# Reading four accumulators at once at the end of a block, in a kernel of a causal convolution and a two-layer squared-ReLU network on one core

## The chip, the core and the metric

One Trainium2 chip, one of its cores. The metric is the device time of one execution in microseconds (us). TensorE (PE) multiplies matrices and writes into PSUM, VectorE (DVE) and ScalarE (ACT) do elementwise work and alone of the engines used here read PSUM, GpSimd (POOL) does a few additions and maxima over partitions, SyncE (SP) and ACT start transfers. Each engine runs its own instructions in their written order and waits for others by semaphores.

## The reference

```python
def _attn_ref(x, weight):             # x (8, 4096, 192), weight (8, 7)
    w = exp(weight - max(weight)); w = w / (sum(w) + 1e-09)
    x_pad = zeros of 6 tokens in front of each sequence, then x
    out[b, s, h, g] = sum over k of w[h, k] * x_pad[b, s + k, h, g]
def _moe_ref(x, w_in, w_out, s, b):   # x (32768, 192), w_in (192, 2048), w_out (2048, 192)
    h = x @ w_in
    r = maximum(h, 0)
    return (s * (r * r) + b) @ w_out
```

A causal convolution of seven taps over the tokens (one set of taps for each of 8 groups of 24 features), and behind it a network with 2048 hidden features whose activation is a scaled square of the ReLU plus an offset.

## The kernel before, in words

Features lie on partitions, tokens along the free dimension. 192 features are 128 ("A") and 64 ("B"). The 32768 tokens are 32 superblocks `n` of 1024 tokens, each two blocks `j` of 512. A block has eight steps `p`, one for each pair of 128 hidden features. All products need nearly full float32 precision, so each operand is split into a high part that TensorE takes exactly and a low rest.

A step has a first layer (`firsts`, L595: 18 matmuls on half of the rows each, two at a time, into the PSUM tile `h`, of which there are two), ACT's ReLU (L627) and square (L634), DVE's cast to the high part `qh` (L643) and DVE's rest (L647 in superblocks 0 and 1; from superblock 2 on, the constant `OLD`, L659, kept in float16). Steps are put into a queue, and the second layer of a step (`second`: L813 in superblock 1, L864 from superblock 2 on) is issued `LAG` = 2 steps behind its first layer. From superblock 2 on the second layer takes only the high parts of the activations; their float16 rests are multiplied once for a block, when its eight steps are through: `rest_B` (L879, 32 matmuls) and `rest_A` (L891, 64 matmuls). These sum into the same four PSUM accumulators of a block, `accs[0]` and `accs[2]` for the A outputs, `accs[1]` and `accs[3]` for the B outputs, and the next block's second layer uses the same four banks: it can't start before they are read.

They are read in `end_of_block`: for B, an ACT instruction (L910) and three DVE instructions (L914), for A one of ACT (L919) and one of DVE (L920). The A tokens of the next block, meanwhile, come from the convolution: DVE multiplies and adds seven taps (L185, L187), ACT copies the high part (L221), DVE subtracts it (L214) and SP swaps the halves of the result with two transfers (L197, L198) into `wA` or `wB`. This work is a generator, cut into pieces, and `convolve(k)` issues the next k of them: `pace` says how many in each step, and `end_of_block` issues three between `rest_B` and the reading of B, and two between `rest_A` and the reading of A. A piece for a tile that is still being read is held back by a gate. If tokens aren't ready when their block begins, `need` issues what is missing on the spot. Each superblock also needs the largest absolute token (L676, then POOL's L673) for its scale, and five small DVE instructions (`unit_of_tokens`).

Superblock 2 is special: before its second layer can run, the second weights `W` are scaled in place (`scale_pair`, L707) and rounded to float16 (`halve_pair`, L712, L713), and its scale needs the column sums and the largest weights that are found in superblock 1 (`column_sums`, `largest_in`, `largest_out`, L557, L676). The outputs of superblocks 0 and the first block of superblock 1 get their bias later (`add_bias`, L583).

Of the kernel before, what the change touches and what calls it, by code (L numbers as in the profile page):

```python
# [15 lines left out]
ALU = mybir.AluOpType  # L16
# [37 lines left out]

RING = 12

WINDOW = 5

GAP = 160

# [15 lines left out]
def conv_attention_then_squared_relu_mlp(  # L76
# [729 lines left out]
    def second_split(n, j, p, qh, ql):  # L806
        accs = accumulators(n, j, p)


        def both(to, w, f, q, start=False, stop=False, cols=P):  # L810
            for i in range(2):
                r = slice(i * HB, (i + 1) * HB)
                nc.tensor.matmul(  # L813
                    accs[to + 2 * i][0:cols], w(f, r), q[r, f % 2, :],
                    start=start and f == 0, stop=stop and f == NF - 1,
                )

        both(1, w_outB, 2 * p, qh, start=True)
        both(1, hiB, 2 * p, ql, cols=HIS)
        both(1, hiB, 2 * p + 1, ql, cols=HIS)  # L820
        both(1, w_outB, 2 * p + 1, qh, stop=True)
        for f in (2 * p, 2 * p + 1):
            both(0, loA, f, qh, start=True)
            both(0, hiA, f, qh)
            both(0, hiA, f, ql, stop=True)
        if p == NPAIR - 1:
            t0 = n * SUP + j * BLK
            early = (n, j) == (1, 0)

            o = {k: hold(n, j, k) for k in range(2)}  # L830
            for k, name in ((1, "oB"), (0, "oA")):
                o[k + 2] = out_tile(name + "2")
                nc.scalar.activation(
                    o[k], accs[k], AF.Identity, scale=sb, bias=0.0 if early else bias[:, k : k + 1]
                )
                nc.scalar.activation(o[k + 2], accs[k + 2], AF.Identity, scale=sb)
            nc.gpsimd.tensor_tensor(o[1], o[1], o[3], op=ALU.add)

            oC = out_tile("oC")[0:DB]
            nc.sync.dma_start(oC, o[1][DB:P])  # L840
            nc.gpsimd.tensor_tensor(o[0], o[0], o[2], op=ALU.add)
            toA, toB = outT[0:P, t0 : t0 + BLK], outT[P:D, t0 : t0 + BLK]
            oB = o[1][0:DB] if early else oC
            if not early:
                nc.sync.dma_start(toA, o[0])
            nc.gpsimd.tensor_tensor(oB, oC, o[1][0:DB], op=ALU.add)
            if early:
                unbiased.extend(((o[0], toA, 0), (oB, toB, 2)))
            else:
                nc.sync.dma_start(toB, oB)  # L850
            del acc[n, j]
# [46 lines left out]
    def next_out():  # L898
        turn[0] += 1
        return out_tile(room[turn[0] % 6])  # L900

    def end_of_block(n, j):

        t0 = n * SUP + j * BLK
        scale = units(n)[1]
        accs = acc[n, j]
        rest_B(n, j)
        convolve(WINDOW - 2)
        oB = next_out()[0:DB]
        nc.scalar.activation(  # L910
            oB, accs[1][DB:P], AF.Identity, scale=scale[DB:P], bias=bias[DB:P, 1:2]
        )
        for a in (accs[1][0:DB], accs[3][0:DB], accs[3][DB:P]):
            nc.vector.scalar_tensor_tensor(oB, a, scale[0:DB], oB, op0=ALU.mult, op1=ALU.add)  # L914
        nc.sync.dma_start(outT[P:D, t0 : t0 + BLK], oB)
        rest_A(n, j)
        convolve(2)
        oA = next_out()
        nc.scalar.activation(oA, accs[0], AF.Identity, scale=scale, bias=bias[:, 0:1])  # L919
        nc.vector.scalar_tensor_tensor(oA, accs[2], scale, oA, op0=ALU.mult, op1=ALU.add)  # L920
        nc.sync.dma_start(outT[0:P, t0 : t0 + BLK], oA)
        del acc[n, j]

    def end_of_last():
# [107 lines left out]
            if next(stream) == "gated":  # L1032
                raise ValueError(what)

    def pace(j, p):
        return 2 if p in (2, 3 + 2 * j) else 1

    steps = [(n, j, p) for n in range(NSUP) for j in range(2) for p in range(NPAIR)]

    def step(n, j, p):  # L1040
        now[0] = 16 * n + 8 * j + p
# [5 lines left out]
            else:  # L1047
                need(n, "A", 1)
        h = first(n, j, p)
        put(n, j, p, squares(h, nc.vector.tensor_copy, *(units(n)[:1] if n >= OLD else ())))  # L1050
        if (n, j) == (1, 1):
            if p < NPAIR - 1:
                column_sums(p + 1)
            largest_out(p)
            convolve(1)
        elif n == 1:
            largest_in(p)
            convolve(2 + p % 2)
        else:
            convolve(pace(j, p))  # L1060
        if (j, p) == (1, NPAIR - 2) and OLD <= n + 1 < NSUP:
            if n + 1 > OLD:
                unit_of_tokens(n + 1)
        if (n, j) == (OLD, 0):
            scale_pair(p)
        if n == OLD and 0 < 8 * j + p <= NPAIR:
            halve_pair(8 * j + p - 1)
        if (n, j, p) == (1, 1, NPAIR - 1):
            unit_of_weights()
            unit_of_tokens(OLD)  # L1070
        if (n, j, p) == (2, 0, 0):
            biases()
        elif n == 2 and p % 2 == 0 and unbiased:
            add_bias()
        if (n, j, p) == steps[-1]:
            return end_of_last()
        while queue and len(queue) > LAG + (
            queue[0][2] == 0 and queue[0][0] <= OLD and queue[0][:2] not in ((1, 0), (OLD, 1))
        ):
            item = queue.pop(0)  # L1080
            second(*item)
# [59 lines left out]
```

## Time and profile before

| | |
|---|---|
| median of 3 runs | 2367.63 us (2366.81 to 2372.58) |
| the profiled execution | 2368.6 us, its span 2366.8 us |
| mean granted TensorE clock | 0.968 of full speed |
| TensorE busy | 2234.1 us, 94% of the span |
| VectorE busy | 1775.0 us, 75% |
| ScalarE busy | 1302.0 us, 55% |
| GpSimd busy | 29.0 us, 1% |

Busy time is the time in which an engine has an instruction in work, summed over the span. A busy TensorE isn't one at its peak: with its clock at one half it is busy for twice as long. Times in the rows further down are counted from the start of the span.

### The profile page before, as it was taken

The numbers are of one execution on the slowest core, as the hardware profiler recorded it, in microseconds if no ns is written. First come the engines' busy times: TensorE is split into PE (matmuls) and PEld (weight loads), VectorE is DVE, ScalarE is ACT, GpSimd is POOL, SyncE is SP. The second block draws the span as 40 slices with busy tenths as digits, with TensorE's granted clock in tenths as the row PEclk, the third lists the DMA queues.
The fourth block names the chain that finished last, engine by engine and source line by source line (L and its number), as shares of the span: only waits on it lengthen the run. The fifth ranks groups of instructions, "written<-read, shape, count | busy, mean of one in ns | idle before, by whom it ended". The sixth has DMA issues, their size and how long they took to land.

```text
span 2366.8 us, 48136 instructions
## 1 busy us (share of the span) xinstructions
PE 2234.1 (94%) x21392; PEld 1766.4 (75%) x21392; DVE 1775.0 (75%) x2391; ACT 1302.0 (55%) x1322; POOL 29.0 (1%) x53
## 2 busy tenths in 40 slices
PE   8999899999999999999999999999999999999999
PEld 6777677777777777767778787786777877777776
DVE  7888678877777677777777777777777677777765
ACT  6747455555555555555455555555555555555554
POOL 0010000000000000000000000000000000000000
PEclk9999999999999999999999999999999999999999
DMA  4112111112112011120111211112112111121110
GB/s 157 32 30 68 42 51 50 48 37 55 39 55 55 19 53 48 46 55 26 46 48 45 55 30 41 51 42 55 32 39 55 39 55 41 30 55 39 50 33 15
DMA packets 41457, 110.00 MB, mean 46 GB/s; under 512 B 6816, under 2 KB 7072, under 8 KB 41248
## 3 DMA queue, kind: packets, MB, share of 16 engines
q1 hardware_dynamic: 32464, 83.03, 13.1%
q10 hardware_dynamic: 8784, 23.89, 3.5%
q8 instruction: 167, 2.74, 0.5%
q14 instruction: 42, 0.34, 0.0%
HBM read 31.66 MB, written 25.17 MB: 24 GB/s over the span
## 4 chain that ended last, share of the span: by engine, by line
PE 75%; DVE 15%; ACT 6%; issue 4%; DMA 1%; DVEq 0%; SPq 0%; POOL 0%; ACTq 0%; POOLq 0%
PE h L595 41%; PE acc L864 26%; PE acc L891 4%; DVE outs L914 3%; ACT q L627 3%; ACT q L634 3%; DVE acc L187 2%; PE acc L879 2%; DVE outs L920 2%; DVE few L676 2%; DVE ql L643 1%; DVE sA L214 1%; DVE sB L214 1%; DMA wA<-sA 1%; DVE acc L185 1%
## 5 line engine op out<-in xcount | busy, mean ns | idle before, releaser
L627 ACT ACTIVATE q<-h,few 128x1024 f32<-128x1024 f32 x480 | 536.5, 1118 | 776.8 <-PE h L595 773.2
L634 ACT ACTIVATE q<-q 128x1024 f32<-128x1024 f32 x512 | 542.9, 1060 | 16.1
L595 PE MATMUL h<-sA,W 64*128 64x512 f32 x3024 | 544.3, 406 | 5.2 <-DVE sA L214 3.8
L595 PE MATMUL h<-wA,W 64*128 64x512 f32 x3024 | 527.4, 395 | 4.0 <-DMA wA<-sA 3.8
L595 PE MATMUL h<-wB,W 64*128 64x512 f32 x1536 | 451.8, 402 | 0.0
L595 PE MATMUL h<-sB,W 64*128 64x512 f32 x1536 | 451.4, 402 | 0.0
L643 DVE CAST ql<-q 128x1024 fp32r<-128x1024 f32 x238 | 165.2, 694 | 364.1 <-ACT q L634 364.1
L595 PEld LDWEIGHTS h<-sA,W 64*128 64x128 f32 x3024 | 377.3, 191 | 73.6 <-issue 24.6
L595 PEld LDWEIGHTS h<-wA,W 64*128 64x128 f32 x3024 | 382.3, 191 | 52.4 <-DMA wA<-sA 7.5
L864 PE MATMUL acc<-qh,W 64*128 64x512 f32 x1920 | 335.4, 406 | 86.6 <-DVE outs L920 86.6
L864 PEld LDWEIGHTS acc<-qh,W 64*128 64x128 f32 x1920 | 231.2, 189 | 135.3 <-DVE outs L920 111.3
L595 PEld LDWEIGHTS h<-wB,W 64*128 64x128 f32 x1536 | 297.2, 194 | 26.1
L595 PEld LDWEIGHTS h<-sB,W 64*128 64x128 f32 x1536 | 298.3, 194 | 23.5 <-issue 0.4
L864 PE MATMUL acc<-ql,W 64*128 64x512 f32 x1900 | 303.4, 386 | 0.0
L659 DVE TENSOR_TENSOR q<-q,qh 128x1024 f16<-128x1024 f32 x240 | 294.1, 1225 | 8.2
L659 DVE TENSOR_TENSOR q<-q,ql 128x1024 f16<-128x1024 f32 x238 | 291.7, 1226 | 8.1
L643 DVE CAST qh<-q 128x1024 fp32r<-128x1024 f32 x251 | 174.6, 696 | 155.7 <-ACT q L634 151.8
L187 DVE SCALAR_TENSOR_TENSOR acc<-xA,share,acc 128x512 f32<-128x512 f32 x372 | 279.0, 750 | 5.4
L864 PEld LDWEIGHTS acc<-ql,W 64*128 64x128 f32 x1900 | 230.2, 184 | 25.0
L864 PE MATMUL acc<-qh,q 64*128 64x512 f32 x960 | 210.5, 398 | 21.5 <-DVE outs L914 21.3
L891 PE MATMUL acc<-q 64*64 64x512 f16 x3840 | 217.4, 376 | 0.0
L864 PE MATMUL acc<-ql,q 64*128 64x512 f32 x950 | 197.3, 389 | 0.0
(161 smaller groups left out, 1692.3 us busy)
## 6 DMA issues: line engine op xcount, KB each, us to landing
wA<-sA SPq DMA_DIRECT2D x124, 256.0 KB, 3.7
wB<-sB SPq DMA_DIRECT2D x62, 256.0 KB, 3.7
outT<-outs SPq DMA_DIRECT2D x59, 256.0 KB, 2.0
xA<-in_xA ACTq DMA_DIRECT2D x23, 515.0 KB, 3.5
outT<-outs SPq DMA_DIRECT2D x62, 128.0 KB, 2.3
xB<-in_xB ACTq DMA_DIRECT2D x30, 259.0 KB, 2.7
q<-in_w SPq DMA_DIRECT2D x7, 768.0 KB, 6.3
xA<-in_xA ACTq DMA_DIRECT2D x7, 512.0 KB, 3.6
```

What stands on the lines that cost most here:

```text
L187: nc.vector.scalar_tensor_tensor(acc, src, w[:, k : k + 1], acc, op0=ALU.mult, op1=ALU.add)
L214: nc.vector.tensor_tensor(s[:, 1, cols], acc, s[:, 0, cols].bitcast(F32), op=ALU.subtract)
L595: nc.tensor.matmul(h[:, i, :], w_in(w, p, chunk[0], rows), chunk[part], start=start, stop=stop)
L627: nc.scalar.activation(q, h, AF.Relu, scale=unit)
L634: nc.scalar.activation(at[0], at[0], AF.Square)
L643: cast(qh, q)
L659: nc.vector.tensor_tensor(ql, q, qh.bitcast(F32), op=ALU.subtract)
L676: nc.vector.tensor_reduce(to, of, axis=axis, op=ALU.max, apply_absolute_value=True)
L864: nc.tensor.matmul(accs[to + 2 * i], w(f, r), qh[r, f % 2, :], start=f == 0 and w is not hiA, stop=whole and f == NF - 1 and w is not loA, ...
L879: nc.tensor.matmul(accs[1 + 2 * k][c], half_B(2 * p + i)[r], ql[r, i, :], start=False, stop=p == NPAIR - 1, skip_group_check=True,)
L891: nc.tensor.matmul(accs[2 * k][c], half_A(f)[r, c], ql[r, f % 2, :], start=False, stop=f == NF - 1, skip_group_check=True,)
L914: nc.vector.scalar_tensor_tensor(oB, a, scale[0:DB], oB, op0=ALU.mult, op1=ALU.add)
```

## The change

At the end of a block `rest_A` follows `rest_B` without anything between, the output instructions come behind both, and one piece of the convolution stands ahead of the last of them, three after it. The other pieces go into the steps, by the table `PACE`. The queue holds the first step of each block for a step longer than before (all blocks but the first of superblock 1; before, that held only in the early superblocks). In superblocks 1 and 2, ACT makes the casts of odd steps. The second block of superblock 1 is read by ACT and DVE, no longer by ACT and POOL. The maxima of the weights, the float16 weights and the late biases move to other steps.

```diff
-WINDOW = 5
+HALVE = {2: (0,), 3: (1,), 4: (2, 3), 5: (4,), 6: (5,), 7: (6,), 8: (7,)}
+
+PACE = (1, 0, 0, 3, 1, 2, 1, 2)
...
-                nc.scalar.activation(o[k + 2], accs[k + 2], AF.Identity, scale=sb)
-            nc.gpsimd.tensor_tensor(o[1], o[1], o[3], op=ALU.add)
+                if early:
+                    nc.scalar.activation(o[k + 2], accs[k + 2], AF.Identity, scale=sb)
+                    nc.gpsimd.tensor_tensor(o[k], o[k], o[k + 2], op=ALU.add)
+                else:
+                    nc.vector.scalar_tensor_tensor(
+                        o[k], accs[k + 2], sb, o[k], op0=ALU.mult, op1=ALU.add
+                    )
...
-            nc.gpsimd.tensor_tensor(o[0], o[0], o[2], op=ALU.add)
...
         rest_B(n, j)
-        convolve(WINDOW - 2)
-        oB = next_out()[0:DB]
+        rest_A(n, j)
+        oB, oA = next_out()[0:DB], next_out()
         nc.scalar.activation(
             oB, accs[1][DB:P], AF.Identity, scale=scale[DB:P], bias=bias[DB:P, 1:2]
         )
         for a in (accs[1][0:DB], accs[3][0:DB], accs[3][DB:P]):
             nc.vector.scalar_tensor_tensor(oB, a, scale[0:DB], oB, op0=ALU.mult, op1=ALU.add)
         nc.sync.dma_start(outT[P:D, t0 : t0 + BLK], oB)
-        rest_A(n, j)
-        convolve(2)
-        oA = next_out()
         nc.scalar.activation(oA, accs[0], AF.Identity, scale=scale, bias=bias[:, 0:1])
+        convolve(1)
         nc.vector.scalar_tensor_tensor(oA, accs[2], scale, oA, op0=ALU.mult, op1=ALU.add)
         nc.sync.dma_start(outT[0:P, t0 : t0 + BLK], oA)
+        convolve(3)
...
-    def pace(j, p):
-        return 2 if p in (2, 3 + 2 * j) else 1
+    def pace(n, p):
+        return PACE[p] + (n == OLD and p in (0, 5))
...
+    def caster(n, p):
+        return nc.scalar.copy if n <= OLD and p % 2 else nc.vector.tensor_copy
...
         if (n, j) == (1, 1):
+            convolve(1)
             if p < NPAIR - 1:
                 column_sums(p + 1)
-            largest_out(p)
-            convolve(1)
+            if p < 4:
+                largest_in(p + 4)
+                largest_out(p)
+            elif p < 6:
+                largest_out(2 * p - 4)
+                largest_out(2 * p - 3)
         elif n == 1:
-            largest_in(p)
-            convolve(2 + p % 2)
+            convolve(3)
+            if p < 4:
+                largest_in(p)
         else:
-            convolve(pace(j, p))
+            convolve(pace(n, p))
...
-        if n == OLD and 0 < 8 * j + p <= NPAIR:
-            halve_pair(8 * j + p - 1)
-        if (n, j, p) == (1, 1, NPAIR - 1):
+        for k in HALVE.get(now[0] - 16 * OLD, ()):
+            halve_pair(k)
+        if (n, j, p) == (1, 1, NPAIR - 2):
             unit_of_weights()
             unit_of_tokens(OLD)
...
-        elif n == 2 and p % 2 == 0 and unbiased:
+        elif n == OLD + 1 and p % 2 == 0 and unbiased:
             add_bias()
...
         while queue and len(queue) > LAG + (
-            queue[0][2] == 0 and queue[0][0] <= OLD and queue[0][:2] not in ((1, 0), (OLD, 1))
+            queue[0][2] == 0 and queue[0][:2] != (1, 0)
         ):
```

What this does to the order, at three places. First TensorE behind the float16 run of a block in the middle of the program (the end of the second block of superblock 16; L891 and L897 are the last matmul of `rest_A`). Before:

```order
L891 MATMUL acc_14018<-q 64x512
L595 MATMUL h<-sA,W 128x512 x6
L595 MATMUL h<-wB,W 128x512
L595 MATMUL h<-sB,W 128x512
...
L595 MATMUL h<-wA,W 128x512 x6
L864 MATMUL acc_14441<-qh,q 128x512
L864 MATMUL acc_14443<-qh,q 128x512
```

and in the changed kernel, where L597 is the first layer and L870 the second:

```order
L897 MATMUL acc_14040<-q 64x512
L597 MATMUL h<-sA,W 128x512 x6
...
L597 MATMUL h<-wA,W 128x512 x6
L597 MATMUL h<-sA,W 128x512 x6
...
L597 MATMUL h<-wA,W 128x512 x6
L870 MATMUL acc_14462<-qh,q 128x512
L870 MATMUL acc_14464<-qh,q 128x512
```

The next block's second layer now begins after two groups of the first layer instead of one; the second layers of its first two steps then follow each other.

Second, VectorE at the same place. Before:

```order
L643 CAST ql<-q 128x1024
L659 TENSOR_TENSOR q<-q,ql 128x1024
L214 TENSOR_TENSOR sA<-acc,sA 128x512
L676 TENSOR_REDUCE few<-xA 128x1
L676 TENSOR_REDUCE few<-few 128x1
L185 TENSOR_SCALAR acc<-xA,share 128x512
L214 TENSOR_TENSOR sB<-acc,sB 128x512
L914 SCALAR_TENSOR_TENSOR outs<-acc_14441,few,outs 64x512
L914 SCALAR_TENSOR_TENSOR outs<-acc_14443,few,outs 64x512 x2
L187 SCALAR_TENSOR_TENSOR acc<-xA,share,acc 128x512 x2
L920 SCALAR_TENSOR_TENSOR outs<-acc_14442,few,outs 128x512
L643 CAST qh<-q 128x1024
```

and in the changed kernel (L920 and L924 read the accumulators, L216 is the low part, L678 the maximum, L187 the first tap):

```order
L645 CAST ql<-q 128x1024
L661 TENSOR_TENSOR q<-q,ql 128x1024
L920 SCALAR_TENSOR_TENSOR outs<-acc_14462,few,outs 64x512
L920 SCALAR_TENSOR_TENSOR outs<-acc_14464,few,outs 64x512 x2
L216 TENSOR_TENSOR sA<-acc,sA 128x512
L924 SCALAR_TENSOR_TENSOR outs<-acc_14463,few,outs 128x512
L678 TENSOR_REDUCE few<-xA 128x1
L678 TENSOR_REDUCE few<-few 128x1
L187 TENSOR_SCALAR acc<-xA,share 128x512
L216 TENSOR_TENSOR sB<-acc,sB 128x512
L645 CAST qh<-q 128x1024
L661 TENSOR_TENSOR q<-q,qh 128x1024
```

The three B readings come first, one low part stands ahead of the A reading, and the rest of the convolution's pieces follow it.

Third, VectorE ahead of superblock 2, whose first tokens are `sA`. Before, their low part stands behind the last column sums of superblock 1:

```order
L557 TENSOR_TENSOR sumA<-sumA,W 128x512
L557 TENSOR_TENSOR sumB<-sumB,WB 128x128
L560 TENSOR_TENSOR sumA<-sumA 128x256
L561 TENSOR_TENSOR sumA<-sumA 128x128
L562 TENSOR_TENSOR sumB<-sumB 128x64
L676 TENSOR_REDUCE few<-W 128x1
L676 TENSOR_REDUCE few<-q 128x1
L214 TENSOR_TENSOR sA<-acc,sA 128x512
```

In the changed kernel it stands ahead of the third of seven column sums (L559 is a column sum, L649 the rest of a step):

```order
L645 CAST qh<-q 128x1024
L649 TENSOR_TENSOR ql<-q,qh 128x1024
L216 TENSOR_TENSOR sA<-acc,sA 128x512
L559 TENSOR_TENSOR sumA<-sumA,W 128x512
L559 TENSOR_TENSOR sumB<-sumB,WB 128x128
L678 TENSOR_REDUCE few<-W 128x1 x2
L678 TENSOR_REDUCE few<-q 128x1
```

The low part moved up by four steps of superblock 1.

## Rows read from the trace of the kernel before

**Rows 1.** Who waited for whom, TensorE alone: total us, times, longest us.

```profile
PE acc L864 <- DVE outs L920: 86.6, 56, 2.1
PE acc L864 <- DVE outs L914: 21.3, 52, 0.7
```

**Rows 2.** Timeline at the end of a block: start, duration (us), engine, line [idle before].

```profile
1199.60 1.23 DVE L659 TENSOR_TENSOR q<-q,ql 128x1024 f16<-128x1024 f32 x1
1199.64 3.62 PE L891 MATMUL acc<-q 64*64 64x512 f16 x64
...
1200.75 0.68 DVE L214 TENSOR_TENSOR sA<-acc,sA 128x512 fp32r<-128x512 f32 x1
1201.35 1.22 DVE L676 TENSOR_REDUCE few<-xA 128x1 f32<-128x1030 f32 x1
...
1203.19 0.96 PE L595 MATMUL h<-sA,W 64*128 64x512 f32 x6
1203.30 0.78 ACT L919 ACTIVATE outs<-acc,bias,few 128x512 f32<-128x512 f32 x1 [2.68 <-PE acc L891]
1203.67 2.37 DVE L914 SCALAR_TENSOR_TENSOR outs<-acc,few,outs 64x512 f32<-64x512 f32 x3
...
1205.57 1.11 ACT L627 ACTIVATE q<-h,few 128x1024 f32<-128x1024 f32 x1 [1.49 <-PE h L595]
1205.96 1.52 DVE L187 SCALAR_TENSOR_TENSOR acc<-xA,share,acc 128x512 f32<-128x512 f32 x2
...
1206.18 0.70 PE L864 MATMUL acc<-qh,q 64*128 64x512 f32 x3 [0.43 <-DVE outs L914]
...
1206.71 1.06 ACT L634 ACTIVATE q<-q 128x1024 f32<-128x1024 f32 x1
1207.52 0.75 DVE L920 SCALAR_TENSOR_TENSOR outs<-acc,few,outs 128x512 f32<-128x512 f32 x1
1208.18 0.68 DVE L643 CAST qh<-q 128x1024 fp32r<-128x1024 f32 x1
...
1208.32 1.19 PE L864 MATMUL acc<-qh,W 64*128 64x512 f32 x7 [1.40 <-DVE outs L920]
```

**Rows 3.** Timeline of TensorE, one step in the last superblock.

```profile
2303.32 0.84 PE L595 MATMUL h<-sA,W 64*128 64x512 f32 x6
...
2305.36 0.62 PE L864 MATMUL acc<-ql,q 64*128 64x512 f32 x4
...
2306.72 0.84 PE L595 MATMUL h<-sA,W 64*128 64x512 f32 x6
```

**Rows 4.** Busy time of the engines in stretches of the span; PEclk is the granted clock.

```profile
core 0: us, PE busy (x) PEld busy (x) DVE busy (x) ACT busy (x) POOL busy (x), PEclk, DMA share, GB/s
123.50:160.20 36.70, 35.16 (x308) 27.71 (x306) 36.04 (x59) 19.87 (x22) 6.48 (x5) 1.00 0.10 26
95.55:210.76 115.21, 107.91 (x894) 85.06 (x894) 100.54 (x162) 68.71 (x87) 11.63 (x9) 0.96 0.17 45
210.76:2354.49 2143.73, 2031.09 (x19777) 1613.70 (x19776) 1591.90 (x2102) 1162.44 (x1148) 16.41 (x36) 0.97 0.16 44
2294.48:2327.21 32.73, 32.73 (x338) 25.12 (x338) 18.87 (x21) 18.98 (x19) 0.00 (x0) 1.00 0.11 29
1281.90:1285.30 3.40, 3.40 (x18) 2.71 (x16) 2.20 (x3) 0.00 (x0) 0.00 (x0) 0.50 0.14 54
162.27:170.23 7.96, 3.99 (x21) 2.04 (x19) 6.68 (x23) 0.06 (x1) 0.50 (x1) 0.72 0.26 66
```

**Rows 5.** Timeline of TensorE where superblock 2 begins.

```profile
164.83 0.73 PE L595 MATMUL h<-sA,W 64*128 64x512 f32 x4 [2.17 <-DVE sA L214]
```

**Rows 6.** Timeline of POOL and VectorE where superblock 1's last outputs are added.

```profile
183.46 1.73 POOL L841 TENSOR_TENSOR q<-q,outs 128x512 f32<-128x512 f32 x1
```

```profile
183.96 1.51 DVE L707 TENSOR_SCALAR W<-W,few 128x512 fp32r<-128x512 f32 x1
...
189.94 0.48 DVE L707 TENSOR_SCALAR W<-W,few 128x512 fp32r<-128x512 f32 x1
```

More of the change, by code (lines that the diff above doesn't have):

```diff
@@ L1049, in step @@
         h = first(n, j, p)
-        put(n, j, p, squares(h, nc.vector.tensor_copy, *(units(n)[:1] if n >= OLD else ())))
+        put(n, j, p, squares(h, caster(n, p), *(units(n)[:1] if n >= OLD else ())))
         if (n, j) == (1, 1):
+            convolve(1)
             if p < NPAIR - 1:
                 column_sums(p + 1)
-            largest_out(p)
-            convolve(1)
+            if p < 4:
[4 more added lines that the diff above has]
+                largest_out(2 * p - 3)
         elif n == 1:
-            largest_in(p)
-            convolve(2 + p % 2)
+            convolve(3)
+            if p < 4:
+                largest_in(p)
         else:
-            convolve(pace(j, p))
+            convolve(pace(n, p))
         if (j, p) == (1, NPAIR - 2) and OLD <= n + 1 < NSUP:
```

## The prediction, made before the changed kernel ran

> **What bounds the kernel now.** I read the waits first. TensorE's longest waits by far are for the two places that read the accumulators, 86.6 us for the A reading and 21.3 us for the B reading, in nearly every one of the 60 blocks of superblocks 2 to 31 [rows 1]. The timeline of one block end shows why [rows 2]. The float16 run of B ends at 1199.64, that of A at about 1203.19. VectorE is free for the B reading at 1200.83 (1199.60 + 1.23), but has pieces of the convolution to do first and begins it at 1203.67. For A, ScalarE's half is done at 1204.08, yet VectorE begins its half at 1207.52: the B readings (2.37) and two taps (1.52) stand ahead of it. TensorE gets on with the B half of the second layer at 1206.18 and with the A half at 1208.32.
>
> What a block costs without such a wait is seen at the end, where no tokens are left to convolve: from the first float16 matmul of block 30/1 to that of block 31/0 TensorE is busy for all of 32.73 us, at a granted clock of 1.00 [rows 4]. Over the 59 intervals between the first and the last such point the time is 2143.73 us, 36.33 for a block, and the granted clock 0.97 [rows 4]. So 59 x (36.33 - 32.73) = 212.7 us lie in waits and what they cause: 107.9 us are waits proper [rows 1]; the clock's missing 3% of 2143.73 us are some 64 us; the other 41 us are TensorE starting again after each pause, and a late start of superblock 3. The clock falls right behind a pause: 1281.90 to 1285.30 runs at 0.50, which is 1.2 GHz, after a block end, and the unbroken stretch at 2.4 GHz [rows 4]. I count the clock's loss as part of the pauses' price.
>
> VectorE is busy for 1591.90 us of those 2143.73 us, 26.98 for a block [rows 4]; in 32.73 us that would be 82%. ScalarE, 1162.44 us, would reach 60%. So TensorE should bound the middle of the program, if the other two come in time.
>
> Ahead of it the picture differs. Between 95.55 and 210.76 TensorE has 894 matmuls; at 2.04 us for 18 [rows 3], 0.113 each, that is 101.3 us of 115.21, so 13.9 us are lost here. But VectorE is busy for 100.54 us of it, and in 123.50 to 160.20 for 36.04 of 36.70 us [rows 4]: there VectorE is the bound.
>
> **The change: end of a block.** The order listing puts the three B readings directly behind the rest. With the durations of rows 2, counted on the same block: B is read from 1200.83 to 1203.20, still inside `rest_A`; the low part follows to 1203.88; ScalarE's A half runs from 1203.30 to 1204.08 as before, and VectorE's A half from there to 1204.85. TensorE has two groups of the first layer to do first, 2 x 2.04 us [rows 3], and comes to the second layer at 1203.19 + 4.08 = 1207.27. Spare: 2.4 us. The wait is gone, not shortened.
>
> What is late next? VectorE's casts. Behind the A reading stand the maximum (1.22), a small one, a first tap and a second low part (together under 2 us, by the 0.68 us of a low part, the longest of the three), so VectorE is free at about 1207.5; in the other variant of the order one more tap (0.75) makes that 1208.2. The ReLU of step 2 runs from 1205.57 to 1206.68, its square to 1207.77 [rows 2], so the cast ends at 1208.9 at worst, and TensorE wants it after two second layers (1.36 each, [rows 3]) and another first layer, at 1207.27 + 2.72 + 2.04 = 1212.0. Spare: 3 us. In step 3 the table puts three taps (2.3 us) behind a cast and a rest (1.9 us); that is 4.2 us in a step of 3.40 us, so the next cast slips by under a microsecond, and the steps behind it carry one or two taps. The queue one step longer costs no transfer and no instruction: it needs `qh` for three waiting steps, and there are six buffers.
>
> Fourteen pieces a block are now issued where fifteen were, and 13.5 are needed (27 for a superblock). By the listing the tokens for a block are ready six or seven steps ahead of it, so `need` has nothing left to do. The transfers on SP keep their order relative to VectorE's work, and each is wanted steps later.
>
> Sum for the 59 intervals: -212.7 us. Bounds: 0 if TensorE waits as long elsewhere, and 212.7 if it never waits.
>
> **The change: superblocks 1 and 2.** Superblock 2 began late because its tokens' low part stood behind all column sums: TensorE waited 2.17 us for it [rows 5] and then for the swap, and a group that takes 2.04 us lasted 7.96 us at a clock of 0.72 [rows 4]. The low part now stands four steps earlier. That stall of 5.9 us and the slow matmuls behind it go, with the cover of four steps of 4.3 us (38 matmuls each) for the swap.
>
> Against that, VectorE is full here. It loses 12 casts of odd steps in this stretch, 12 x 0.68 = 8.2 us [rows 2], and ScalarE, busy for 68.71 of 115.21 us [rows 4], has room for them (at the square's 1.06 us, 12.7 us). It gains two readings of accumulators, 1.5 us at the A reading's 0.75. POOL's three additions for superblock 1's last block go; while one of them ran, a scaling took 1.51 us where another took 0.48 [rows 6], so three such collisions give back about 3.1 us. VectorE's 100.54 us become some 90.7 us, in 101.3 us if TensorE never waited. That fits only if spread evenly, and the listing doesn't: until the scale of superblock 2 is known, nearly all of it stands in eight steps that were already full, and only four of the odd casts are in them. I take VectorE to reach superblock 2 about 3 us late, and the new readings of superblock 1's accumulators, behind a scaling and a rest, to hold TensorE for about 3 us more. Of 13.9 us I book 7.8, with 0 and 13.9 as bounds.
>
> The Trainium skill (SBUF — State Buffer, section "SBUF: two separate sides") says that VectorE and GpSimd share a pair of ports that one of them holds for a whole instruction while the other is blocked. By it each of the three additions would block for up to the 1.73 us of rows 6, some 5.2 us in all, and the sum would be 2 us lower. The row shows 1.03 us, which I use.
>
> The spread of `halve_pair` and the late biases move ScalarE work of the same length into steps where ScalarE is at most 60% busy; booked at nothing, and if that cover were gone, a bias instruction is under the 0.78 us of the A reading [rows 2], six times.
>
> **Sum.** The profiled execution took 2368.6 us, 1.8 us more than its span, and 1 us more than the median of the three runs, 2367.63. 2368.6 - 212.7 - 7.8 = 2148.1. I predict 2148 us, 9.3% less. Its own range is 2138 to 2165: lower if the early part loses nothing, higher if a block keeps 0.2 to 0.3 us.
>
> **Rivals.**
> *A part of the wait stays.* VectorE runs in order at 82%, and one late instruction delays a cast or a reading; the spare of 2.4 us is from one block. For it: VectorE's full stretch above. Against it: the listing repeats the same two orders. If half of what a block loses stayed, 2148 + 106 = 2254 us; at a quarter, 2201.
> *The clock stays.* If the pauses aren't what lowers it, 64 us remain: 2212 us. Against it, the last blocks run at 1.00 without pauses [rows 4]. The Trainium skill (TensorE: Matmul & The Clock Gate, "Why this matters for your kernels") puts the fall down to longer pauses than those of rows 2; by that rule this rival would be right, but the trace has the falls just behind such pauses.
> *Slower: the tokens come late.* If pieces moved into steps were too few or gated, each block would begin as superblock 2 did, 5.9 us late [rows 4]: 2148 + 59 x 5.9 = 2496 us. It is slower than before from 3.7 us a block on. Against it, the low parts' places in the listing.
> *No effect.* If the second layer were held by something else than the readings, say the casts, it would stay at about 2360 us. Against it, TensorE's A half starts at 1208.32, right at the end of the A reading (1207.52 + 0.75) [rows 2].
>
> **Chances.** The forecast 0.72, a part of the wait 0.16 (up to 2215 in half of these), the clock 0.07, slower 0.02, no effect 0.02, the rest 0.01. The range 2138 to 2215 holds the forecast, the clock and half of the partial waits, some 8 in 10 when the forecast's own error is counted. A measurement of this kernel can tell some 0.3%, 7 us, from no change: faster 0.96, same 0.02, slower 0.02.
>
> **What would show it.** In the changed profile TensorE's waits for the reading lines should be near zero and the first float16 matmul of a block should follow that of the block before in 32.7 to 33 us; the granted clock should be 1.00 from superblock 3 on; VectorE's share should rise to about 82%. Superblock 2's first layer should start without waiting for `sA`, and the first float16 matmul should come at about 203 us instead of 210.76. The prediction is wrong if TensorE waits for a cast in steps 3 to 5, if low clocks stand in unbroken stretches, or if superblocks 1 and 2 lose more than 14 us.

## The result, and the profile after

The changed kernel takes 2137.35 us (median of 4 runs, 2137.07 to 2137.51), against 2369.93 us for the kernel before (4 runs): a ratio of 0.902, 95% interval 0.900 to 0.9035. That is 9.8% less, where 9.3% and 2148 us were predicted, and 0.65 us below the low end of the range, 2138. The profiled execution took 2137.4 us, with a span of 2135.6.

The page of the changed kernel, parts 1 and 2 (busy time of each engine; TensorE's busy tenths and granted clock in 40 slices):

```profile
PE 2121.9 (99%) x21392; PEld 1628.2 (76%) x21392; DVE 1765.7 (83%) x2377; ACT 1311.1 (61%) x1336; POOL 28.5 (1%) x51
PE   8999999999999999999999999999999999999999
PEclk9999999999999999999999999999999999999999
```

TensorE's waits, all that the view lists (for whom, on what: total us, times, longest us):

```profile
PE h L259 <- DVE q L418: 5.5, 1, 5.5
PE acc L407 <- POOL q L375: 1.0, 1, 1.0
PE acc L870 <- DVE q L709: 0.8, 1, 0.8
PE h L597 <- DVE W L343: 0.6, 1, 0.6
PE h L597 <- DVE bias L578: 0.4, 1, 0.4
```

The two readings that it waited for 108 times [rows 1] are gone from the list, and nothing that happens once in a block has come in. What is left are five single waits, three of them ahead of superblock 1.

The end of a block in the middle, as a timeline of the changed kernel (start, us, engine, line; L897 is `rest_A`, L597 the first layer, L870 the second, L920 and L924 the readings of B and A by DVE):

```profile
1344.98 1.22 DVE L661 TENSOR_TENSOR q<-q,ql 128x1024 f16<-128x1024 f32 x1
1345.01 3.62 PE L897 MATMUL acc<-q 64*64 64x512 f16 x64
1346.12 2.37 DVE L920 SCALAR_TENSOR_TENSOR outs<-acc,few,outs 64x512 f32<-64x512 f32 x3
1348.57 0.96 PE L597 MATMUL h<-sA,W 64*128 64x512 f32 x6
1348.67 0.78 ACT L922 ACTIVATE outs<-acc,bias,few 128x512 f32<-128x512 f32 x1 [2.68 <-PE acc L897]
1349.48 0.75 DVE L924 SCALAR_TENSOR_TENSOR outs<-acc,few,outs 128x512 f32<-128x512 f32 x1 [0.99 <-ACT outs L922]
...
1352.78 0.62 PE L870 MATMUL acc<-qh,q 64*128 64x512 f32 x4
1353.23 1.07 PE L870 MATMUL acc<-qh,W 64*128 64x512 f32 x8
```

B is read inside `rest_A`, as the walk on [rows 2] had it. The order has turned round: before, DVE was late and ACT's half had long been done; now DVE waits 0.99 us for ACT. The A reading ends at 1350.23 and TensorE begins the second layer at 1352.78.

The stretches that answer to [rows 4] (columns as there): from superblock 1's start to the first float16 matmul, from there to the last such point, and the interval from block 30/1 to 31/0.

```profile
94.44:197.46 103.02, 101.76 (x895) 83.03 (x894) 93.49 (x157) 77.92 (x94) 9.41 (x7) 1.00 0.17 45
197.46:2123.26 1925.80, 1925.80 (x19779) 1477.89 (x19777) 1589.63 (x2093) 1162.57 (x1155) 18.18 (x36) 1.00 0.19 49
2063.25:2095.97 32.72, 32.72 (x338) 25.12 (x336) 18.86 (x21) 18.86 (x19) 0.00 (x0) 1.00 0.11 29
```

In the second row TensorE is busy for every one of 1925.80 us at full clock. Of the 59 intervals 57 are 32.73 us, the first is 33.1 and the last 27.29.

### The profile page after: what moved, and what is told of

Same layout as the page of the kernel before. It is cut to its first block, busy times and chain, and to the rows that moved or that the text cites. A ratio compares the mean times of both kernels' runs of the same rounds, so it can differ in the third digit from the quotient of the medians.

```text
span 2135.6 us, 48042 instructions
## 1 busy us (share of the span) xinstructions
PE 2121.9 (99%) x21392; PEld 1628.2 (76%) x21392; DVE 1765.7 (83%) x2377; ACT 1311.1 (61%) x1336; POOL 28.5 (1%) x51
## 4 chain that ended last, share of the span: by engine, by line
PE 97%; DVE 2%; ACT 1%; issue 1%; DVEq 0%; POOL 0%; POOLq 0%; ACTq 0%
PE h L597 49%; PE acc L870 30%; PE acc L897 10%; PE acc L885 5%; PE acc L815 1%; PE h L259 0%; PE acc L781 0%; PE acc L787 0%; PE acc L789 0%; PE acc L788 0%; DVE acc L189 0%; PE acc L780 0%; DVE few L678 0%; ACT q L636 0%; ACT q L629 0%
## 5 line engine op out<-in xcount | busy, mean ns | idle before, releaser
L597 PE MATMUL h<-sA,W 64*128 64x512 f32 x3024 | 432.5, 391 | 0.4 <-DVE bias L578 0.4
L597 PE MATMUL h<-sB,W 64*128 64x512 f32 x1536 | 430.6, 387 | 0.0
L597 PE MATMUL h<-wB,W 64*128 64x512 f32 x1536 | 430.6, 387 | 0.0
L597 PE MATMUL h<-wA,W 64*128 64x512 f32 x3024 | 425.7, 386 | 0.0
L597 PEld LDWEIGHTS h<-sA,W 64*128 64x128 f32 x3024 | 278.8, 184 | 80.7 <-issue 24.6
L597 PEld LDWEIGHTS h<-wA,W 64*128 64x128 f32 x3024 | 283.9, 184 | 60.1 <-DMA wA<-sA 0.7
L597 PEld LDWEIGHTS h<-sB,W 64*128 64x128 f32 x1536 | 282.6, 184 | 30.8 <-issue 0.4
L597 PEld LDWEIGHTS h<-wB,W 64*128 64x128 f32 x1536 | 282.6, 184 | 30.7
L870 PE MATMUL acc<-qh,W 64*128 64x512 f32 x1920 | 256.9, 386 | 0.0
L870 PE MATMUL acc<-ql,W 64*128 64x512 f32 x1900 | 254.8, 386 | 0.0
L897 PE MATMUL acc<-q 64*64 64x512 f16 x3840 | 217.4, 376 | 0.0
L870 PEld LDWEIGHTS acc<-qh,W 64*128 64x128 f32 x1920 | 180.1, 184 | 37.7
L870 PEld LDWEIGHTS acc<-ql,W 64*128 64x128 f32 x1900 | 178.8, 184 | 37.2
L897 PEld LDWEIGHTS <-q 64*64 64x64 f16 x3840 | 112.7, 107 | 94.4
L870 PE MATMUL acc<-qh,q 64*128 64x512 f32 x960 | 148.1, 386 | 0.0
```

The source lines that it names most:

```text
L597: nc.tensor.matmul(h[:, i, :], w_in(w, p, chunk[0], rows), chunk[part], start=start, stop=stop)
L870: nc.tensor.matmul(accs[to + 2 * i], w(f, r), qh[r, f % 2, :], start=f == 0 and w is not hiA, stop=whole and f == NF - 1 and w is not loA, ...
L897: nc.tensor.matmul(accs[2 * k][c], half_A(f)[r, c], ql[r, f % 2, :], start=False, stop=f == NF - 1, skip_group_check=True,)
```

## Where the prediction's 10.7 us are

The spans differ by 2366.8 - 2135.6 = 231.2 us; the prediction booked 212.7 + 7.8 = 220.5.

| stretch | before | after | gain | booked |
|---|---|---|---|---|
| start to superblock 1's first matmul | 95.55 | 94.44 | 1.1 | 0 |
| to the first float16 matmul | 115.21 | 103.02 | 12.2 | 7.8 |
| the 59 intervals | 2143.73 | 1925.80 | 217.9 | 212.7 |
| the rest | 12.3 | 12.3 | 0 | 0 |

The first line is scatter: the head is the same code, and in the runs below the same point lies between 93.8 and 95.5 us. The other two are terms of the sum that were mis-sized. The one on the blocks could have been read from the kernel before, in a row that the prediction doesn't show, the last interval (31/0 to 31/1):

```profile
2327.21:2354.49 27.28, 27.28 (x290) 20.62 (x288) 14.78 (x17) 15.59 (x15) 0.00 (x0) 1.00 0.05 16
```

Behind the last block there is no next one, so two first layers (2 x 2.04) are missing from this interval, and a second layer (1.36) is put behind the float16 run: 5.44 us less. This interval is 27.28 us long before and 27.29 after. The other 58 were (2143.73 - 27.28) / 58 = 36.49 us each, not 36.33, and gave 58 x (36.49 - 32.73) = 218.1 us. The first of them, in which superblock 3 begins late, was 44.07 us long and is 33.10 now: 11.0 of the 218 us lie there.

## The experiments

Theory 1 is that of the prediction: the late readings stop TensorE, the lost clock and the restarts are the price of those stops, and the early part gives back some 12 us. Its rivals are named with each run. Medians are of 4 or 5 runs, with the kernel before at 2368 us beside them.

**Both block parts undone, only the early part kept (early_only).** The old end of a block, the old table of pieces from superblock 3 on and the old queue rule:

```diff
-        rest_A(n, j)
-        oB, oA = next_out()[0:DB], next_out()
+        convolve(WINDOW - 2)
+        oB = next_out()[0:DB]
...
+        rest_A(n, j)
+        convolve(2)
+        oA = next_out()
```

Expected:

> Both parts at the end of a block undone from superblock 2 on (old order of the readings, old pieces in the steps from superblock 3 on, old rule of the queue); the changes of superblocks 1 and 2 stay. Theory 1 (the gain is the 59 intervals' 212.7 us and about 14 us ahead of them, and the two add): 2137 + 213 = 2350 us. Rival (a fast early part alone shifts the phase of the later blocks and gives back part): under 2335 or over 2365 us.

Measured: 2351.99 us (2351.24 to 2352.6), ratio 0.993, interval 0.9915 to 0.9945. TensorE's waits of this kernel, where L922 and L928 are the B and the A reading:

```profile
PE acc L872 <- DVE outs L928: 85.1, 56, 2.0
PE acc L872 <- DVE outs L922: 21.5, 53, 1.1
```

They are those of [rows 1] again, and the clock over the blocks is 0.97 again. The first float16 matmul comes 103.03 us behind superblock 1's start, as in the changed kernel, so the 12.2 us belong to the early part. The 59 intervals take 2139.57 us, 4.2 less than before: the first one is 35.03 us long instead of 44.07, and the others lose 4.9 again. So nearly all of the blocks' 218 us goes with the two block parts, but the end of superblock 3's late start belongs to the early part.

**Only the old order and pace, with the queue's delay kept (late_read).** The edit above without the old queue rule. Expected:

> The changed kernel with the other part undone: the end of a block and the pieces of the convolution in the steps (from superblock 3 on) are as before, three pieces ahead of the B reading and two ahead of the A reading; the second layer of a block stays a step later. Theory 1: the readings end as late as before, for A about 5.1 us behind the float16 run, and TensorE's A half now comes at 4.08 + 0.45 = 4.5 us, so 0.5 us a block is left: 2137 + 59 x 0.5 = 2167 us if the clock holds, up to 2230 us if it falls as before. Theory 2 (the delay alone does nearly nothing, since the reading's place is all that counts): a block stays near 36 us, 2300 us or more.

Measured: 2175.92 us (2175.23 to 2175.99), ratio 0.919, 0.917 to 0.920. The wait that stands in the list, and the place of one of them in the timeline (L872 is the second layer, L928 the A reading):

```profile
PE acc L872 <- DVE outs L928: 8.8, 25, 0.7
1208.39 0.61 PE L872 MATMUL acc<-qh,q 64*128 64x512 f32 x4
1208.76 0.75 DVE L928 SCALAR_TENSOR_TENSOR outs<-acc,few,outs 128x512 f32<-128x512 f32 x1
1208.84 0.39 PE L872 MATMUL acc<-qh,W 64*128 64x512 f32 x1
...
1209.57 1.19 PE L872 MATMUL acc<-qh,W 64*128 64x512 f32 x7 [0.34 <-DVE outs L928]
1210.37 0.85 PE L872 MATMUL acc<-ql,q 64*128 64x512 f32 x4
```

The delay alone leaves 38 us of the blocks' 218: the 59 intervals take 1963.79 us, 38.0 more than after the change, of which 8.8 are waits in the list, while the granted clock over them is 1.00. In an interval with the 0.34 us wait the two second layers around it take 3.36 us instead of 2.72, and the last second layer before `rest_B` takes 1.67 instead of 1.45. So 29.2 us, about 0.5 for a block, lie beside the listed waits. The starts of the matmuls show where. The matmuls run in pairs, one on each half of the rows, and a pair starts every 0.22 us; in the changed kernel's timeline above, the eight of an A half stand in one row from 1353.23 on. Here the first of them starts at 1208.84 and its partner, which needs the bank that DVE reads, at 1209.57. The partner is 0.73 us late, but the list has 0.34, since it counts from the end of the matmul ahead, 0.39 us after that one's start, and it leaves out the shortest (0.08 us in the block behind this one). From start to start 53 blocks are late by 0.57 us in the mean, 30.4 us in all, and a late block loses about 0.15 us on top. The theory's range held, and so did its 0.5 us for a block; it is the list that shows too little.

**The second layer not a step later (no_delay).**

```diff
-            queue[0][2] == 0 and queue[0][:2] != (1, 0)
+            queue[0][2] == 0 and queue[0][0] <= OLD and queue[0][:2] not in ((1, 0), (OLD, 1))
```

Expected:

> The changed kernel with one part undone: the queue's rule is the old one, so from superblock 2's second block on a block's second layer comes after one group of the first layer, not two. Theory 1 (the reading's place on VectorE is what counts; the step of delay is spare): the A reading ends some 1.7 us after the float16 run, and TensorE's A half comes at 2.04 + 0.45 = 2.5 us after it, so it never waits: 2137 us, within 0.3%, TensorE's waits for the reading near 0. Theory 2 (both parts are needed, since the reading is late in many blocks): a wait of 0.5 to 1 us a block comes back, 2137 + 59 x 0.5 to 1 = 2166 to 2196 us, with the clock falling up to 2260 us.

Measured: 2137.41 us (2136.7 to 2138.49), ratio 0.9025, 0.901 to 0.904; no reading among TensorE's waits. With the new order the step of delay isn't needed.

**The A reading three taps later (taps_first, taps_first_no_delay).**

```diff
-        convolve(1)
+        convolve(4)
         nc.vector.scalar_tensor_tensor(oA, accs[2], scale, oA, op0=ALU.mult, op1=ALU.add)
...
-        convolve(3)
```

The second of the two has the old queue rule as well. Expected:

> The changed kernel with the A reading behind all four pieces of the convolution at a block's end instead of one: three taps later, 3 x 0.66 = 2.0 us. Theory 1 (the readings have the spare that the prediction's walk counted, 2.4 us; in the changed profile an A reading ends at 1350.23 and TensorE comes to the A half at about 1353.4, 3.2 us): TensorE waits for no reading, the time is 2137 to 2140 us. Theory 2 (the spare of the walk isn't there, since VectorE is slower in other blocks or the taps delay the casts of steps 2 and 3): waits of 0.3 us and more in a block, the time 2150 to 2200 us.

> The same later A reading, and the second layer not a step later: TensorE comes to the A half one first layer (2.04 us) earlier. Theory 1 (spare of 3.2 us in the changed kernel, so 3.2 - 2.0 - 2.04 = -0.9 us here): TensorE waits for the A reading in nearly every block, 0.7 to 1.3 us in some 58 blocks, with about 0.5 us more for each to start again, 60 to 105 us in all: 2200 to 2245 us. Theory 2 (the step of delay buys nothing in any order, as the run without it alone would suggest): no wait, 2137 to 2140 us.

Measured: 2137.38 us (2136.97 to 2138.58) with the delay, and 2199.55 us (2199.15 to 2200.55), ratio 0.928, 0.927 to 0.930, without it. The latter's longest list entry for TensorE, and its blocks (columns as above):

```profile
PE acc L870 <- DVE outs L924: 33.8, 52, 1.1
197.00:2180.00 1983.00, 1949.11 (x19736) 1479.34 (x19734) 1581.62 (x2091) 1165.99 (x1153) 18.67 (x36) 1.00 0.18 48
```

So the spare is real and about as large as counted. It covers the taps (in taps_first the A reading ends 1.9 us later in the median block), or one first layer of 2.04, but not both. Counted from start to start as in late_read, TensorE's A half is then 1.00 us late in 54 blocks, where 0.9 was expected; the list shows 0.65. The 59 intervals take 1987.9 us, 62.1 more than after the change: 54.2 of lateness and about 0.15 for each of 54 stops, at a clock of 1.00. The expectation added 0.5 us to each wait for starting again, of which only 0.15 came, so the kernel comes out just under the range.

**Only the block parts (blocks_only).** The kernel before, with the new end of a block, the new queue rule and `PACE` from superblock 3 on. Expected:

> The kernel before with the two parts at the end of a block (readings behind the float16 run, pieces in the steps from superblock 3 on, second layer a step later); superblocks 1 and 2 otherwise as before. Theory 1 (the parts add): the early 13 to 14 us are lost, and superblock 3's late start is some 8 us of the 212.7: 2150 to 2160 us. Rival (the early part's gain needed the block part, or the reverse): under 2145 or over 2170 us.

Measured: 2182.1 us (2179.23 to 2184.53), ratio 0.921, 0.920 to 0.923: some 25 us above what was expected. TensorE's waits name something new (L595 is the first layer, `sA` and `wA` the tokens):

```profile
PE h L595 <- DVE sA L214: 8.8, 3, 3.3
PE h L595 <- DMA wA<-sA: 6.7, 11, 1.8
PE h L595 <- ACT sA L221: 4.2, 1, 4.2
```

They stand where superblocks 2 to 6 begin, and the intervals in which 3 to 6 do are 43.10, 42.03, 42.15 and 38.83 us long; 51 of the others are 32.73. This is the rival "the tokens come late", at its place but for a few superblocks: a superblock issues 28 pieces and needs 27, so the convolution gains one piece in each until its lead suffices. By the code, superblocks 1 and 2 ask for 56 pieces in this kernel, 58 in the kernel before and 64 in the changed one: with 14 pieces a block from superblock 2 on and the old superblock 1, it has the smallest lead of the three.

**The lead without the two extra pieces (no_extra).** Superblock 2 has two more pieces in each block; without them:

```diff
-        return PACE[p] + (n == OLD and p in (0, 5))
+        return PACE[p]
```

Expected:

> The changed kernel without the two extra pieces of the convolution in each block of superblock 2 (4 of 32 pieces), so that from there on tokens are four pieces later: the low part of superblock 3's tokens stands in step 7 of the block before, as in the kernel with the block parts alone, where TensorE waited at the start of superblocks 3 to 6; with 28 pieces a superblock for 27 it gains one piece on the tokens in each. Theory 1 (the lead of the tokens is what that kernel lacked, and these pieces give it): TensorE waits 2 to 5 us at the start of superblock 3 and less at the starts of the next one or two, each with a stretch at half clock, and the time is 2143 to 2160 us. Theory 2 (that kernel lost its time through the other early parts, not through the lead): no wait at the start of a superblock, 2137 to 2139 us.

Measured: 2150.57 us (2148.07 to 2151.87), ratio 0.907, 0.906 to 0.909. TensorE's waits of this kernel for tokens, and the interval in which superblock 3 begins:

```profile
PE h L597 <- DVE sA L216: 3.7, 1, 3.7
PE h L597 <- DMA wA<-sA: 3.3, 4, 1.8
196.20:238.77 42.57, 37.86 (x339) 28.09 (x338) 25.76 (x37) 24.55 (x26) 0.50 (x1) 0.88 0.17 47
```

Four pieces in the whole program, under 3 us of VectorE's time, are worth 13.2 us by the medians, and by the trace 42.57 - 33.1 = 9.5 in this interval and 38.91 - 32.73 = 6.2 two further on, less 1.0 us that superblock 2 saves. So 13 us of the whole gain hang on this lead, and the prediction doesn't mention the four pieces. Theory 1 held.

**The casts of superblocks 1 and 2 back on VectorE (casts_dve).**

```diff
-        return nc.scalar.copy if n <= OLD and p % 2 else nc.vector.tensor_copy
+        return nc.vector.tensor_copy
```

Expected:

> The changed kernel, with the odd steps' casts of superblocks 1 and 2 back on VectorE: 12 more casts of 0.69 us between superblock 1's start and the first float16 matmul of superblock 2, four of them in the eight full steps. Theory 1 (VectorE has room in the early part: in the changed profile it is busy for 93.53 of 101.95 us, and an instruction begins about 0.08 us before the one ahead of it ends, so that 12 casts take some 7.3 us): the casts fit nearly, TensorE loses 0 to 3 us and only behind the full steps, and the time is 2137 to 2141 us. Theory 2 (as in the prediction's step: VectorE is saturated until superblock 2 and what is added there is added to the time): the first float16 matmul comes 3 to 8 us later, 2140 to 2146 us, with waits for casts or for the scale in the full steps.

Measured: 2142.82 us (2142.43 to 2143.58), ratio 0.904, 0.903 to 0.9055. The early stretch, and two entries of TensorE's waits that the changed kernel doesn't have:

```profile
94.14:202.71 108.57, 103.05 (x894) 81.28 (x894) 101.91 (x169) 65.87 (x82) 7.99 (x7) 1.00 0.16 43
PE h L576 <- DVE sumB L564: 2.5, 1, 2.5
PE acc L815 <- DVE ql L649: 1.4, 2, 1.1
```

The first float16 matmul comes 108.57 - 103.02 = 5.5 us later. Here theory 1, as I stated it, was wrong and theory 2 right: VectorE had no room for 12 casts; the change had just made as much as was needed.

**Superblock 1's second block read by ScalarE and GpSimd (pool_adds).**

```diff
-                    nc.vector.scalar_tensor_tensor(
-                        o[k], accs[k + 2], sb, o[k], op0=ALU.mult, op1=ALU.add
-                    )
+                nc.scalar.activation(o[k + 2], accs[k + 2], AF.Identity, scale=sb)
```

(and the three GpSimd additions again). Expected:

> The changed kernel, with superblock 1's second block read again by ScalarE alone and added up by GpSimd (in place of two VectorE readings of accumulators). Theory 1 (the two readings are done before TensorE wants the accumulators, so they cost it nothing; what they buy is that GpSimd's additions don't run beside VectorE's scaling of the weights): the time stays or gets longer by 0 to 3 us, 2137 to 2140 us, with VectorE's scalings near 176 to 186 us drawn out from 0.48 to about 1.5 us each. Theory 2 (the prediction's step, the two readings hold TensorE for about 3 us): the first float16 matmul comes up to 3 us earlier and the time falls to about 2134 to 2136 us.

Measured: 2137.42 us (2137.13 to 2138.83), ratio 0.902, 0.901 to 0.903; the early stretch takes 103.43 us, 0.4 more. The two VectorE readings hold TensorE for nothing (in the changed kernel they are over before its second layer wants the banks, see below), and the three additions that they replace cost nearly nothing here: two of VectorE's instructions beside them are drawn out (a scaling to 1.38 us, a rest to 2.19), where it has time to spare.

**The old places in superblock 1 (old_spread).** Pieces of the convolution, maxima and the unit as before. Expected:

> The changed kernel, with the convolution's pieces, the maxima and the unit of superblock 2 in superblock 1 at the places that they had before; casts on ScalarE, readings on VectorE and both changes of the blocks are kept. The low part of superblock 2's tokens stands again behind all column sums. Theory 1 (of the 12 to 13 us that the early part gave back, the place of that low part is the largest share): TensorE waits 3 to 6 us for superblock 2's tokens, runs some us at half clock behind it, and the time is 2142 to 2148 us. Theory 2 (the casts and the readings moved off VectorE and GpSimd gave most of it, since without 4 casts the same queue is 2.7 us shorter): the low part comes early enough, the wait is under 2 us, and the time is 2137 to 2140 us.

Measured: 2157.55 us (2155.98 to 2158.2), ratio 0.910, 0.909 to 0.912, outside either range. Its early stretch is 108.27 us, 5.3 longer: TensorE waits for superblock 2's tokens and their swap (0.49, 1.73 and 0.69 us). That part was expected. Not expected were two longer intervals, 41.51 and 37.98 us, where superblocks 3 and 4 begin: the old places issue four pieces fewer in superblock 1, and the lead is missing as in no_extra. The three kernels agree on it: with 60 pieces in superblocks 1 and 2 (no_extra, old_spread) the 59 intervals take 15.7 and 13.7 us more than with 64, with 56 (blocks_only) 35.0.

**A piece moved out of a full step (extra_later).** In superblock 2's first block the extra piece stands in the third step instead of the first:

```diff
-        return PACE[p] + (n == OLD and p in (0, 5))
+        return PACE[p] + (n == OLD and (j, p) in ((0, 2), (0, 5), (1, 0), (1, 5)))
```

Expected:

> The changed kernel with superblock 2's extra piece of the convolution in its first step moved to its third, where VectorE has only a cast and a rest. Theory 1 (what the early part still loses are waits behind a full VectorE: 0.43 us for the bias in the first step and 0.83 us for a scaled weight, and without that piece the first float16 matmul came 1.0 us earlier): 0.4 to 1.0 us less, 2136.4 to 2137.0 us. Theory 2 (those waits end with ScalarE and the scalings, whose time the piece doesn't set): no difference.

Measured: 2136.96 us (2136.4 to 2137.98), against 2137.35: the early stretch is 102.69 us (94.79 to 197.48) instead of 103.02. The wait for the bias is gone from TensorE's list, and the one for a scaled weight is 0.7 us. Over six traces with the changed kernel's early part (the changed kernel, early_only, late_read, no_delay and the two of the later A reading) this stretch is 103.02 to 103.10 us, so the 0.33 us in this one trace agree with theory 1, if at less than its 0.4. The two kernels' times overlap, and by them the gain can't be told from no change.

Two things were not undone by themselves: the other places of the float16 weights (`HALVE`) and those of the late biases. The prediction booked them at nothing; no run here shows what they are worth.

## Why the prediction was nearly right, and where it wasn't

**What bounds it.** Right. The readings' waits were the cause: with them the clock's losses and the restarts go too, and with both block parts undone all three are back (early_only). The 41 us that it put down to TensorE starting again are in part only the list's way of counting (late_read): a stop itself costs about 0.15 us beyond its length.

**The block's end.** The walk was right. Its spare was 2.4 us; the profile after shows 1352.78 - 1350.23 = 2.55 to the start of the second layer, and it is the same, within 0.01 us, in 58 blocks: in the block shown no low part stands ahead of the A reading, in others one does, but either way the reading begins when ACT's half is done. The second layer's A half, which alone has to wait, begins at 1353.23, so 3.0 us are spare there. That agrees with taps_first_no_delay, where 1.9 and 2.04 us are taken from them and 1.0 us is lacking. The casts of steps 2 and 3 hold nothing up.

**"59 x (36.33 - 32.73) = 212.7 us".** The first step that failed, by 5.2 us. The mean was taken over all 59 intervals and each compared with 32.73, though the last is a shorter one in either kernel. The term measured 217.9. The bound on the gain that followed ("212.7 if it never waits") was too low for the same reason, and so the range's low end was too high. In mechanism this step had a hole as well: it counts superblock 3's late start in the 212.7, but nothing in it ends that start. The early pieces do; with the block parts but fewer early pieces that interval is still 43.10 us (blocks_only) or 42.57 (no_extra).

**The early part, "Of 13.9 us I book 7.8".** The second step that failed, by 4.4 us: the term measured 12.2. The cost terms were the main error: "I take VectorE to reach superblock 2 about 3 us late, and the new readings of superblock 1's accumulators ... to hold TensorE for about 3 us more". Neither came. In the eight full steps TensorE is busy throughout (first line, columns as in [rows 4]). VectorE's timeline of the changed kernel shows the readings (L842) and the first cast of superblock 2 (164.72), with two rows from a full step (L678, L649):

```profile
132.32:164.72 32.40, 32.40 (x292) 26.40 (x292) 30.41 (x68) 22.63 (x25) 6.89 (x5) 1.00 0.09 22
144.06 0.87 DVE L678 TENSOR_REDUCE few<-W 128x1 f32<-128x384 f32 x2
144.84 0.27 DVE L678 TENSOR_REDUCE few<-q 128x1 f32<-128x128 f32 x1
145.04 1.21 DVE L649 TENSOR_TENSOR ql<-q,qh 128x1024 fp32r<-128x1024 f32 x1
...
164.72 0.69 DVE L645 CAST qh<-q 128x1024 fp32r<-128x1024 f32 x1 [0.41 <-ACT bias L577]
...
171.37 1.40 DVE L842 SCALAR_TENSOR_TENSOR q<-acc,sb,q 128x512 f32<-128x512 f32 x2
```

An instruction begins before the one ahead of it has ended: 144.84 is 0.09 us ahead of 144.06 + 0.87. Over the eight full steps, 132.3 to 164.7, 66 VectorE instructions have durations of 34.7 us in sum and are busy for 30.4: whoever adds durations counts 4.3 us that don't pass. That is larger than the 3 us that I took VectorE to be late and may be where they came from; the prediction gives no working for them. VectorE is in fact at the cast on time: there it waits 0.41 us for ACT's part of the bias, and TensorE waits 0.4 us for the bias behind it. The readings are over at 172.77, ahead of superblock 2's second layer, which TensorE begins at 173.12 without a pause. That VectorE has no room to spare there was right (casts_dve); undone one at a time, the casts give 5.5 us, the places 5.3, the readings 0.4, in sum 11.2 of the 12.2.

**GpSimd's additions.** "Three such collisions give back about 3.1 us" was also too much, an error the other way: pool_adds costs 0.4 us, with the 1.40 us of VectorE's two readings saved.

**The rivals.** No part of the wait stayed. "The clock stays" was wrong: granted clock 1.00 over all blocks. The Trainium skill (TensorE: Matmul & The Clock Gate, "Why this matters for your kernels") puts the fall down to longer pauses than those of rows 1; by that rule the clock should have stayed low without them. The trace disagrees: with the pauses gone, none of them over 2.1 us [rows 1], the stretches at 0.50 [rows 4] are gone too. "The tokens come late" was given 0.02 as a whole; as a mechanism it is the nearest danger of this change, since it costs 13 us when four pieces are left out and some 35 us with the block parts alone. The listing of the changed kernel, which the prediction cited against it, was the right evidence.

## What to carry to other kernels

When a mean over repeated intervals is compared with an ideal one, look at the first and last interval by themselves, since a shorter one that the change can't touch hides part of the loss in the mean. On an engine that is the bound, walk with the distances from start to start in the timeline and not with durations; the same goes for waits, which a list can count too short. A producer that just keeps pace needs a lead built up ahead of the loop, and a few extra pieces early can be worth more than a whole step of delay in the loop.

## What the runs showed of the hardware

A wait of TensorE costs more than the list of waits shows, even where the clock doesn't fall, but little more than its length from start to start: about 0.15 us for each stop, both where the stops are 0.57 us in the mean (late_read) and where they are 1.00 (taps_first_no_delay). Most of the 0.15 is in the first pair of matmuls behind the stop: the next pair starts 0.33 us after it instead of 0.22. The longer last layer ahead of the next float16 run, some 23 us later (1.67 us for a second layer instead of 1.45), isn't a second price. The stop splits a pair, all matmuls behind it run in pairs shifted by one, and the last one ahead of the float16 run goes alone, 0.22 us.

With one listed wait of up to 1.1 us in a block the granted clock stayed at 1.00 (2.4 GHz) throughout (taps_first_no_delay), while the kernel before, with two waits in most blocks (up to 0.7 and 2.1 us [rows 1]), had stretches at 0.50 (1.2 GHz). It doesn't take two: in the kernel before, one block has a single wait, and the clock fell behind it all the same (timeline, and stretches with columns as in [rows 4]):

```profile
547.32 1.53 PE L864 MATMUL acc<-qh,W 64*128 64x512 f32 x7 [2.12 <-DVE outs L920]
536.90:548.00 11.10, 8.98 (x126) 5.52 (x127) 9.81 (x15) 5.29 (x6) 0.51 (x1) 1.00 0.39 94
548.00:551.40 3.40, 3.40 (x20) 2.65 (x18) 2.54 (x3) 0.00 (x0) 0.00 (x0) 0.50 0.78 204
```
